# One product in place of two for z: the sum of phi(k) folded to 64 partitions, its bf16 high and low parts stacked

## Chip, cores, metric

The kernel runs on one core of a Trainium2 chip. The metric is the device time of one execution in microseconds. Before and after a change are compared by runs on the same chip. All runs told here are of one core and "fast" (within 1.5% of the fastest run of the same kernel).

Engines in the profile: PE is TensorE's matmul, PEld its weight load, DVE is VectorE, ACT is ScalarE, POOL is GpSimd, SP is SyncE, which issues the DMAs.

## The reference

Linear attention with 32 heads of 16, and a gated FFN, both of the same x (2048 x 512), mixed by a sigmoid gate. What matters here is the sum z of phi(k) over all tokens, which only the denominator uses:

```python
phi = lambda t: jnp.where(t > 0, t + 1, jnp.exp(t)) + 1e-6
pq, pk = phi(q), phi(k)
kv = jnp.einsum("bhsd,bhse->bhde", pk, v)
z = jnp.einsum("bhsd->bhd", pk)                       # the sum over tokens
num = jnp.einsum("bhqd,bhde->bhqe", pq, kv)
den = jnp.einsum("bhqd,bhd->bhq", pq, z)[..., None] + 1e-6
o = num / den
# a = o @ wo;  b = (silu(x @ w1) * (x @ w3)) @ w2;  out = g * a + (1 - g) * b
```

## The kernel before

The order of PE's instructions is set by hand, in the order of the text. All other engines are ordered automatically at compile time: each engine works through one queue in order, but which instruction stands where in that queue is chosen by a scheduler.

Four PSUM buffers in a pool called psM, used in rotation, carry the k tiles, the four q tiles of the first block, two r_ps (remainder of the FFN) and then gate_ps and up_ps of each FFN chunk. So r_ps 0 and 1 take the buffers of q tiles 0 and 1, the first gate_ps takes that of q tile 2, and the first up_ps that of q tile 3.

The names in the timelines: ScalarE reads r_ps as thr and upr. In an FFN chunk ScalarE makes th from gate_ps, VectorE makes gs from th and gate_ps, and then hT from gs and up_ps; with gs and hT the two buffers come free. For the denominator GpSimd multiplies pq by z_sb to qz, VectorE sums qz to den and inverts it to rden, GpSimd makes pqn from pq and rden, and a DMA transposes it to pqT, which the first o_ps reads.

```python
psM = ctx.enter_context(tc.tile_pool(name="psM", bufs=4, space=bass.MemoryType.PSUM))
# ... (cut: loads and constants)
def phi(dst, ps):                                     # frees ps only with its last line
    e = work.tile([P, D], BF16, tag="phi_e", name="phi_e")
    e_ins = nc.scalar.activation(out=e[:], in_=ps, func=ACT.Exp)
    em = work.tile([P, D], BF16, tag="phi_m", name="phi_m")
    nc.vector.tensor_scalar(out=em[:], in0=e[:], scalar1=1.0, scalar2=1e-6, op0=ALU.min, op1=ALU.add)
    nc.vector.scalar_tensor_tensor(out=dst, in0=ps, scalar=0.0, in1=em[:], op0=ALU.max, op1=ALU.add)
    return e_ins
# ... (cut)
def emit_k_phi(k_ps, t):                              # pks: partial sums, one per partition
    e_ins = phi(pk_sb[:, t, :], k_ps[:])
    if t == 0:
        nc.gpsimd.tensor_copy(pks[:], pk_sb[:, t, :])
    else:
        nc.gpsimd.tensor_add(pks[:], pks[:], pk_sb[:, t, :])
# ... (cut: transposes, k tiles, XP products, the q, r, FFN and output emitters)
emit_q(0, 2, psM, "mm")
emit_q(0, 3, psM, "mm")
emit_rem(0, 0, psM, "mm")
emit_rem(0, 1, psM, "mm")
# ... (cut: kvT_ps and its masked copy)
pks_hi = consts.tile([P, D], BF16, name="pks_hi")
nc.gpsimd.tensor_copy(pks_hi[:], pks[:])
pks_lo = consts.tile([P, D], BF16, name="pks_lo")
nc.gpsimd.tensor_sub(pks_lo[:], pks[:], pks_hi[:])
for fc in range(FC):                                  # ten FFN chunks of the first block
    emit_ffn(0, fc)
    if fc == 0:
        z_ps = psX.tile([P, D], FP32, tag="XP1", name="z_ps")
        nc.tensor.matmul(z_ps[:], lhsT=ones_b[:], rhs=pks_hi[:], start=True, stop=False)
        nc.tensor.matmul(z_ps[:], lhsT=ones_b[:], rhs=pks_lo[:], start=False, stop=True)
        nc.scalar.activation(out=z_sb[:], in_=z_ps[:], func=ACT.Copy)
    if 1 <= fc <= TPB:
        emit_den(0, fc - 1)                           # qz on GpSimd, its reduction on VectorE
    if fc == TPB + 1:
        emit_norm(0)                                  # rden on VectorE, pqn on GpSimd, pqT by DMA
    # ... (cut: W_ps after chunks 1 and 3, in the buffers XP0 to XP3)
```

## Time and profile before

| | value | where it is read |
|---|---|---|
| time | 181.27 us (181.25 to 181.48, 3 runs) | the runs |
| span of the profiled run | 179.2 us | profile page |
| PE busy | 174.8 us, 98% | profile page |
| one 128x512 product | 0.216 us (0.86 us for four) | chain of waits |
| stretch from the third q tile to the first o_ps | 24.37 us | timeline of PE |

The stretch in the last row is the part of the program that the change touches. I measure it from the start of the products of q tiles 2 and 3 (one line of the timeline) to the start of the first o_ps. It leaves out what comes before: the stretch starts between 35.07 and 36.04 us in the twelve traces, and where I looked the difference arose in the first 12 us, in waits of PE for the loads of x.

The profile page of before, first part (busy microseconds, share of the span, instructions):

```profile
span 179.2 us, 2463 instructions
PE 174.8 (98%) x884; PEld 83.7 (47%) x884; DVE 118.0 (66%) x202; ACT 65.8 (37%) x123; POOL 61.4 (34%) x69
```

VectorE's last step of phi, which frees the PSUM buffer, for tiles 1 and 2:

```profile
36.62 0.68 DVE L143 SCALAR_TENSOR_TENSOR pq<-q_ps,phi_m 128x512 bf16<-128x512 f32 x1
37.53 0.69 DVE L143 SCALAR_TENSOR_TENSOR pq<-q_ps,phi_m 128x512 bf16<-128x512 f32 x1
```

Tile 1 is free at 36.62 + 0.68 = 37.30 us, and the second r_ps, eight products after the first, follows at about 37.5 us (36.83 and half of 1.36). So its slack is 0.2 us. Tile 2 is free at 38.22 us and the first gate_ps starts at 39.08: 0.9 us.

The same stretch cut in three by busy time of each engine (first the r products and kvT, then the ten FFN chunks, then q and r of the next block up to the first o_ps):

```profile
35.10:39.08 3.98, 3.98 (x41) 3.04 (x40) 3.91 (x9) 3.22 (x8) 1.94 (x3) 1.00 0.31 97
39.08:57.93 18.85, 18.81 (x90) 8.40 (x88) 16.81 (x34) 9.02 (x17) 9.72 (x10) 1.00 0.19 34
57.93:59.47 1.54, 1.54 (x13) 1.06 (x12) 1.34 (x2) 0.48 (x1) 0.00 (x0) 1.00 0.17 35
```

The columns are the window, its length, then PE, PEld, DVE, ACT and POOL, the granted clock, DMA share and GB/s. In the chunks VectorE works 16.81 of 18.85 us, and PE loses about 0.3 us to it. One reason is visible in VectorE's timeline, before, at the start of the chunks:

```profile
41.61 0.69 DVE L317 TENSOR_TENSOR hT<-up_ps,gs 128x512 bf16<-128x512 f32 x1
43.31 0.69 DVE L222 TENSOR_REDUCE den<-qz 128x32 f32<-128x512 f32 x1 [1.01 <-POOL qz L219]
43.91 0.68 DVE L314 SCALAR_TENSOR_TENSOR gs<-th,gate_ps 128x512 bf16<-128x512 bf16 x1
```

The scheduler put the first den ahead of gs of chunk 1. VectorE waits 1.01 us for qz, and for the last 0.4 us of that the gs could have run (its th ends at 42.90 us); it starts at 43.91.

### The profile page before, as it was taken

To read this page: it belongs to the slowest core of one execution; us is meant where nothing else is said; L and a number is where in the kernel's file an instruction comes from. 1 tells how busy PE (TensorE), PEld (TensorE's weight loads), DVE (VectorE), ACT (ScalarE), POOL (GpSimd) and SP (SyncE) were. 2 spreads that over 40 slices of the span, in tenths; PEclk is the share of its full clock that TensorE was granted. 3 is DMA by queue.
4 is the path that set the end of the run, shared out by engine and by line. 5 is a ranking of instruction groups with operands and counts; after the bars stand their busy time and mean duration, and the time that the engine had idled before them with its cause. 6 is when DMAs were issued, how large, how long until landed. Compare 5 with 4: busy or idle time off the path is not lost.

```text
span 179.2 us, 2463 instructions
## 1 busy us (share of the span) xinstructions
PE 174.8 (98%) x884; PEld 83.7 (47%) x884; DVE 118.0 (66%) x202; ACT 65.8 (37%) x123; POOL 61.4 (34%) x69
## 2 busy tenths in 40 slices
PE   8899999999999999999999999999999999999993
PEld 3344444474444545444445444444545444444463
DVE  1388667897998837398787374977764669776000
ACT  3442322566523334343324343332443323331221
POOL 5177765646453323253003232620032328100000
PEclk9999999999999999999999999999999999999999
DMA  5999999901006011115000101240001013300011
GB/s 165 244 242 239 294 334 398 348 28 26 9 11 110 0 44 33 44 42 104 0 0 4 44 31 42 59 90 5 0 7 54 19 59 67 61 0 0 29 46 45
DMA packets 29340, 15.14 MB, mean 84 GB/s; under 512 B 20656, under 2 KB 28304, under 8 KB 29328
## 3 DMA queue, kind: packets, MB, share of 16 engines
q1 hardware_dynamic: 29328, 14.98, 31.2%
q8 instruction: 7, 0.11, 0.3%
q14 instruction: 5, 0.04, 0.1%
HBM read 8.42 MB, written 2.10 MB: 59 GB/s over the span
## 4 chain that ended last, share of the span: by engine, by line
PE 93%; DVE 2%; DMA 2%; SPq 1%; ACT 0%; issue 0%; DVEq 0%
PE o_ps L344 19%; PE gate_ps L301 18%; PE up_ps L307 18%; PE o_ps L335 8%; PE q_ps L211 8%; PE XP L198 8%; PE k_ps L178 6%; PE r_ps L235 3%; PE o_ps L339 2%; DMA x_sb<-in_A_x_dram 2%; PE k L178 2%; DVE hT L317 1%; DVE gs L314 1%; PE kvT_ps L402 0%; SPq L86 0%; PE W_ps L429 0%
## 5 line engine op out<-in xcount | busy, mean ns | idle before, releaser
L301 PE MATMUL gate_ps<-xT,w_sb 128*128 128x512 bf16 x160 | 41.1, 379 | 0.0
L307 PE MATMUL up_ps<-xT,w_sb 128*128 128x512 bf16 x160 | 41.1, 379 | 0.0
L219 POOL TENSOR_TENSOR qz<-pq,z_sb 128x512 f32<-128x512 bf16 x16 | 18.5, 1162 | 60.2 <-DVE pq L143 58.6
L312 ACT ACTIVATE th<-gate_ps 128x512 bf16<-128x512 f32 x40 | 23.9, 597 | 38.2 <-PE gate_ps L301 37.8
L344 PE MATMUL o_ps<-w_sb,hT 128*128 128x512 bf16 (+2 forms) x180 | 37.5, 355 | 0.0
L314 DVE SCALAR_TENSOR_TENSOR gs<-th,gate_ps 128x512 bf16<-128x512 bf16 x40 | 27.3, 682 | 5.9 <-ACT th L312 5.6
L317 DVE TENSOR_TENSOR hT<-up_ps,gs 128x512 bf16<-128x512 f32 x40 | 27.7, 691 | 3.8
L140 DVE TENSOR_SCALAR phi_m<-phi_e 128x512 bf16<-128x512 bf16 x32 | 14.4, 450 | 23.0 <-ACT phi_e L138 22.9
L344 PEld LDWEIGHTS <-hT 128*128 128x128 bf16 x180 | 16.8, 97 | 17.9
L307 PEld LDWEIGHTS <-w_sb 128*128 128x128 bf16 x160 | 15.6, 98 | 19.0 <-issue 0.2
L301 PEld LDWEIGHTS <-w_sb 128*128 128x128 bf16 x160 | 15.6, 98 | 18.9 <-issue 0.3
L349 ACT ACTIVATE o_out<-o_ps,omg 128x512 bf16<-128x512 f32 (+2 forms) x17 | 11.1, 656 | 30.4 <-PE o_ps L344 30.4
L284 POOL TENSOR_TENSOR pqn<-pq,rden 128x512 bf16<-128x512 bf16 x16 | 16.6, 1056 | 14.1 <-DVE rden L277 11.7
L188 POOL TENSOR_TENSOR pks<-pks,pk_sb 128x512 f32<-128x512 f32 x15 | 17.6, 1173 | 8.9 <-DVE pk_sb L143 8.4
L222 DVE TENSOR_REDUCE den<-qz 128x32 f32<-128x512 f32 x16 | 10.9, 684 | 8.9 <-POOL qz L219 8.8
L335 PE MATMUL o_ps<-W_sb,pqT 128*128 128x512 bf16 (+2 forms) x72 | 16.8, 355 | 0.0
L211 PE MATMUL q_ps<-wq_sb,xT 128*128 128x512 bf16 x64 | 16.3, 379 | 0.0
L198 PE MATMUL XP<-pk_sb,x_sb 128*128 128x512 bf16 x64 | 16.1, 379 | 0.0
L138 ACT ACTIVATE phi_e<-k_ps 128x512 bf16<-128x512 f32 x12 | 7.2, 597 | 15.3 <-PE k_ps L178 15.3
L178 PE MATMUL k_ps<-wk_sb,xT 128*128 128x512 bf16 x48 | 12.3, 379 | 0.0
L138 ACT ACTIVATE phi_e<-q_ps 128x512 bf16<-128x512 f32 x16 | 9.6, 597 | 7.0 <-PE q_ps L211 6.8
L143 DVE SCALAR_TENSOR_TENSOR pq<-q_ps,phi_m 128x512 bf16<-128x512 f32 x16 | 11.1, 691 | 0.5
(59 smaller groups left out, 116.5 us busy)
## 6 DMA issues: line engine op xcount, KB each, us to landing
w_sb<-in_B_w_dram SPq DMA_DIRECT2D x3, 1280.0 KB, 9.6
out_dram<-o_out SPq DMA_DIRECT2D x15, 128.0 KB, 1.9
x_sb<-in_A_x_dram SPq DMA_DIRECT2D x3, 512.0 KB, 4.3
wk_sb<-in_A_wqkv_dram SPq DMA_DIRECT2D x2, 256.0 KB, 3.0
wq_sb<-in_A_wqkv_dram SPq DMA_DIRECT2D x1, 512.0 KB, 4.9
wv_sb<-in_A_wqkv_dram SPq DMA_DIRECT2D x1, 512.0 KB, 6.6
wo_sb<-in_A_wo_dram SPq DMA_DIRECT2D x1, 512.0 KB, 10.5
x_sb<-in_A_x_dram SPq DMA_DIRECT2D x2, 128.0 KB, 2.7
```

The source lines that it names most:

```text
L178: nc.tensor.matmul(k_ps[:], lhsT=xT[:, kc, t * P : (t + 1) * P], rhs=wk_sb[:, kc, :], start=(kc == 0), stop=(kc == KC - 1),)
L188: nc.gpsimd.tensor_add(pks[:], pks[:], pk_sb[:, t, :])
L198: nc.tensor.matmul(XP_ps[dc][:], lhsT=x_sb[:, t, dc * P : (dc + 1) * P], rhs=pk_sb[:, t, :], start=(t == 0), stop=(t == NT - 1),)
L211: nc.tensor.matmul(q_ps[:], lhsT=xT[:, kc, ts_tok], rhs=wq_sb[:, kc, :], start=(kc == 0), stop=(kc == KC - 1),)
L219: nc.gpsimd.tensor_tensor(out=qz[:], in0=st[tb, "pq"][:, tt, :], in1=z_sb[:], op=ALU.mult)
L301: nc.tensor.matmul(gate_ps[:], lhsT=w1_sb[:, kc, fsl], rhs=xT[:, kc, tok_sl], start=(kc == 0), stop=(kc == KC - 1),)
L307: nc.tensor.matmul(up_ps[:], lhsT=w3_sb[:, kc, fsl], rhs=xT[:, kc, tok_sl], start=(kc == 0), stop=(kc == KC - 1),)
L312: nc.scalar.activation(out=th[:], in_=gate_ps[:], func=ACT.Tanh, scale=0.5)
L314: nc.vector.scalar_tensor_tensor(out=gs[:], in0=th[:], scalar=1.0, in1=gate_ps[:], op0=ALU.add, op1=ALU.mult)
L317: nc.vector.tensor_tensor(out=st[tb, "hT"][:, fc, :], in0=up_ps[:], in1=gs[:], op=ALU.mult)
L335: nc.tensor.matmul(o_ps[:], lhsT=st[tb, "pqT"][:, c, tsl], rhs=W_sb[:, c, a:b], start=(c == 0), stop=False,)
L344: nc.tensor.matmul(o_ps[:], lhsT=st[tb, "hT"][:, fc, tsl], rhs=w2_sb[:, fc, a:b], start=False, stop=(fc == FC - 1),)
```

## The change

The intent is to save one of two z products on PE. The 128 partial sums per column are first added in pairs, in fp32, to 64; their bf16 high part then fills partitions 0 to 63 of one tile and their low part partitions 64 to 127, so one product with ones sums both. Two copies from one half of the partitions to the other are needed, and are given to ScalarE. As the chain is longer, z comes after chunk 2 instead of chunk 0, and den and norm move two chunks with it.

```diff
-    pks_hi = consts.tile([P, D], BF16, name="pks_hi")
-    nc.gpsimd.tensor_copy(pks_hi[:], pks[:])
-    pks_lo = consts.tile([P, D], BF16, name="pks_lo")
-    nc.gpsimd.tensor_sub(pks_lo[:], pks[:], pks_hi[:])
+    HP = P // 2
+    pks_up = consts.tile([HP, D], FP32, name="pks_up")
+    nc.scalar.activation(out=pks_up[:], in_=pks[HP:P, :], func=ACT.Copy)
+    pks_f = consts.tile([HP, D], FP32, name="pks_f")
+    nc.gpsimd.tensor_add(pks_f[:], pks[0:HP, :], pks_up[:])
+    pks_hl = consts.tile([P, D], BF16, name="pks_hl")
+    nc.gpsimd.tensor_copy(pks_hl[0:HP, :], pks_f[:])
+    pks_lo = consts.tile([HP, D], BF16, name="pks_lo")
+    nc.gpsimd.tensor_sub(pks_lo[:], pks_f[:], pks_hl[0:HP, :])
+    nc.scalar.activation(out=pks_hl[HP:P, :], in_=pks_lo[:], func=ACT.Copy)
     for fc in range(FC):
         emit_ffn(0, fc)
-        if fc == 0:
+        if fc == 2:
             z_ps = psX.tile([P, D], FP32, tag="XP1", name="z_ps")
-            nc.tensor.matmul(z_ps[:], lhsT=ones_b[:], rhs=pks_hi[:], start=True, stop=False)
-            nc.tensor.matmul(z_ps[:], lhsT=ones_b[:], rhs=pks_lo[:], start=False, stop=True)
+            nc.tensor.matmul(z_ps[:], lhsT=ones_b[:], rhs=pks_hl[:], start=True, stop=True)
             nc.scalar.activation(out=z_sb[:], in_=z_ps[:], func=ACT.Copy)
-        if 1 <= fc <= TPB:
-            emit_den(0, fc - 1)
-        if fc == TPB + 1:
+        if 3 <= fc <= TPB + 2:
+            emit_den(0, fc - 3)
+        if fc == TPB + 3:
             emit_norm(0)
```

## The prediction

> **What bounds the kernel.** TensorE. The page gives PE busy 174.8 us of a 179.2 us span (98%); the chain of waits is PE for 93% of the span, at a granted clock of 0.998 (view of cores). The measured 181.27 us is 2.1 us more than the span. In the chain four 128x512 matmuls take 0.86 us, so one costs 0.216 us; the 379 ns that the groups list overlaps the neighbours. The Trainium skill, "TensorE: Matmul & The Clock Gate", section "Wait — 56ns, not 53.3ns?", has 215.7 ns start to start; this trace agrees.
>
> In the timeline of the first block's ten FFN chunks (39.2 to 58.1 us) PE is packed but for about 0.3 us: up_ps of chunk 4 starts 0.95 us after its gate_ps instead of 0.865, and gate_ps of chunk 6 comes 1.07 us after the product before it. The chain shows why: VectorE (hT, gs, rden from 47.5 to 51.0 us) frees PSUM buffers late, since four den reductions (0.68 us each, 0.6 apart) and the normalisation (1.4 us) come on top of 1.39 us of gs and hT per 1.73 us chunk.
>
> **Removed.** One of the two z products: 0.216 us of PE, on the critical path. That is the only sure gain.
>
> **Added, off PE.** Two ScalarE copies of 64x512 (0.60 us each, as every 128x512 ACTIVATE here) and a GpSimd add of 64x512 (I expect 1.15 us, as for 128 partitions: each lane keeps its 512 elements). The cast (0.61) and the subtraction (1.16) stay as long. The chain from pks (complete at 35.3 us) was 1.85 us long and ended at 37.2; z waited to 40.8 only for its place in PE's order. It becomes 0.6 + 1.15 + 0.61 + 1.16 + 0.6, with hand-overs 4.5 us, ending near 40 us if each step starts at once, near 44 us if ScalarE and GpSimd (two hr products, 1.05 us) are busy. The product now comes at about 44.7 us. I expect PE not to wait for it.
>
> **Moved.** z_sb lands at about 45.7 instead of 42.0 us, so qz, den, rden and pqn move 3.7 us later. VectorE's extra work meets chunks 3 to 7 instead of 1 to 5. The same load on the same four PSUM buffers: PE's 0.3 us of stalls probably moves two chunks later and changes by 0.3 us either way. Before, pqT's first transpose was issued at 52.3 us and landed 2.4 us later, 4.7 us before o_ps first read it (59.4). Afterwards I expect landing at 58.4 and need at 59.1: 0.7 us is left. Later slices are needed 4 us apart and made 1.1 us apart.
>
> ScalarE's queue is in order: if the last copy (waiting for GpSimd) stands ahead of a th, that th comes up to 1 to 2 us late, against about 1.2 us of slack before PE lacks a PSUM buffer. That could give back 0.2 to 0.7 us.
>
> **Prediction.** 181.27 - 0.22 + about 0.05 for the risks: 181.1 us, 8 in 10 between 180.8 and 181.7. Faster by over 2%: 0.005; within 2%: 0.985; slower by over 2%: 0.01.
>
> **What would show it.** Right: one z product fewer, PE busy down about 0.2 us; PE not waiting for pks_hl; copies near 0.6 us and the half-partition add near 1.15 us; den and rden 3.5 to 4 us later; o_ps not waiting for pqT. Wrong: half-partition operations clearly shorter; PE idle before z, before gate_ps of chunks 3 to 8, or before o_ps.
>
> **What would make it wrong.** A th stuck behind the last copy for over 1.5 us; pqT landing after 59.1 us, which adds its lateness once; the first block's chunks stalling over 0.3 us longer because den and rden bunch up; or the other engines' order changing elsewhere (they are scheduled automatically).

## More of the kernel before

The timeline of PE, before, around the q tiles (start, duration, engine, line, operation, out<-in, shapes, count; a bracket at the end would give idle time and its releaser):

```profile
35.10 1.89 PE L211 MATMUL q_ps<-wq_sb,xT 128*128 128x512 bf16 x8
36.83 1.53 PE L235 MATMUL r_ps<-wr_sb,xT 128*128 128x193 bf16 x16
38.19 1.05 PE L402 MATMUL kvT_ps<-XP_sb,wv_sb 128*128 128x128 bf16 x16
39.08 1.03 PE L301 MATMUL gate_ps<-xT,w_sb 128*128 128x512 bf16 x4
```

No bracket: PE has no wait here. The timeline of ScalarE over the same time:

```profile
34.44 0.60 ACT L138 ACTIVATE phi_e<-q_ps 128x512 bf16<-128x512 f32 x1 [1.13 <-PE q_ps L211]
...
36.16 0.60 ACT L138 ACTIVATE phi_e<-q_ps 128x512 bf16<-128x512 f32 x1
37.02 0.60 ACT L138 ACTIVATE phi_e<-q_ps 128x512 bf16<-128x512 f32 x1 [0.27 <-PE q_ps L211]
```

These are the exponentials of q tiles 1, 2 and 3; each starts as soon as its tile is there.

## The result and the profile after

The time after is 183.97 us (median of 4 runs, 183.64 to 184.18), beside 181.38 us before (4 runs, 181.25 to 181.73). The ratio is 1.0138 with a 95% interval of 1.0122 to 1.0154. Ratios here are the mean time of one kernel's fast runs over that of the other's fast runs of the same rounds, so they are not quite the ratios of the medians. The change makes the kernel about 2.5 us slower, where 0.2 us less was predicted, and the time lies outside the stated range.

The profile page, first part, after:

```profile
span 182.5 us, 2464 instructions
PE 175.0 (96%) x883; PEld 83.5 (46%) x883; DVE 117.1 (64%) x202; ACT 66.6 (37%) x125; POOL 62.7 (34%) x70
```

One PE instruction is gone, as meant, but the span grew by 3.3 us. PE's busy time did not fall, so busy time alone would not have shown the saved product either. The timeline of PE, after, for the same place:

```profile
35.59 1.89 PE L211 MATMUL q_ps<-wq_sb,xT 128*128 128x512 bf16 x8
37.32 0.84 PE L235 MATMUL r_ps<-wr_sb,xT 128*128 128x193 bf16 x8
39.16 0.84 PE L235 MATMUL r_ps<-wr_sb,xT 128*128 128x193 bf16 x8 [1.00 <-DVE pq L143]
39.84 1.05 PE L402 MATMUL kvT_ps<-XP_sb,wv_sb 128*128 128x128 bf16 x16
42.04 1.02 PE L301 MATMUL gate_ps<-xT,w_sb 128*128 128x512 bf16 x4 [1.15 <-DVE pq L143]
```

Two waits of over 1 us have appeared, both for pq, that is for the PSUM buffers of q tiles 1 and 2. The idle time in brackets is a little less than the loss, because the ends of matmuls are modelled. From start to start, the r products take 39.84 - 37.32 = 2.52 us instead of 1.36, and from kvT_ps to gate_ps it is 2.20 us instead of 0.89: a loss of 1.16 and of 1.31 us. Both come well before the z product. The timeline of ScalarE, after, says why:

```profile
35.79 0.63 ACT L413 ACTIVATE pks_up<-pks 64x512 f32<-64x512 f32 x1 [2.00 <-POOL pks L188]
36.33 0.57 ACT L138 ACTIVATE phi_e<-q_ps 128x512 bf16<-128x512 f32 x1
...
39.69 0.63 ACT L420 ACTIVATE pks_hl<-pks_lo 64x512 bf16<-64x512 bf16 x1 [1.82 <-POOL pks_lo L419]
40.34 1.08 ACT L138 ACTIVATE phi_e<-q_ps 128x512 bf16<-128x512 f32 x2
```

The first new copy stands ahead of the exponential of q tile 1, and the second ahead of those of tiles 2 and 3, although the text has both after all four. ScalarE sits idle for 2.00 and 1.82 us, waiting for GpSimd. For the last 0.86 us of the first wait (q tile 1 is there at about 34.93 us, if it takes 1.07 us from the start of its products as before) and for all of the second, finished q tiles wait behind it.

VectorE's timeline shows that the first loss has a second part:

```profile
36.94 0.98 DVE L140 TENSOR_SCALAR phi_m<-phi_e 128x512 bf16<-128x512 bf16 x1 [0.88 <-ACT phi_e L138]
...
38.44 0.67 DVE L143 SCALAR_TENSOR_TENSOR pq<-q_ps,phi_m 128x512 bf16<-128x512 f32 x1
```

The phi_m of tile 1 took 0.62 us before and takes 0.98 us here, while GpSimd works on pks_f (36.50 to 37.76 us; e4 comes back to such overlaps). So my estimate is that about 0.36 of the 1.16 us comes through GpSimd's work on the fold; no run tests that part alone. The chain of waits of after follows the whole path (start, duration, what; "issue" pieces and some steps between are left out):

```profile
34.61 1.16 POOL pks L188
35.79 0.64 ACT pks_up L413
36.50 1.27 POOL pks_f L415
38.51 1.16 POOL pks_lo L419
40.34 0.60 ACT phi_e L138
41.30 0.70 DVE pq L143
42.04 1.02 PE gate_ps L301 x4
```

The fold's chain ends with the second copy at 40.32 us and feeds a product that comes at 47.65 us, so its data are 7 us early. It has become part of the critical path through a queue and not through its data. Note that the chain reaches gate_ps without passing through r_ps: the first stall of PE lies beside it.

The stretch in three windows, after:

```profile
35.59:42.04 6.45, 4.31 (x41) 3.09 (x40) 3.67 (x7) 4.40 (x11) 3.18 (x4) 1.00 0.24 76
42.04:60.89 18.85, 18.67 (x86) 8.28 (x86) 17.05 (x35) 9.31 (x19) 7.46 (x8) 1.00 0.04 9
60.89:62.68 1.79, 1.71 (x13) 1.00 (x12) 1.46 (x4) 0.65 (x2) 1.25 (x2) 1.00 0.38 75
```

The first window is 2.47 us longer. The ten chunks take 18.85 us as before, although a product of 0.22 us is gone: the later den and norm cost that much more in waits for VectorE. The last is 0.25 us longer, as the first o_ps waits for pqT. In all 27.09 instead of 24.37 us: 2.72 us more. The profiled span has another 0.5 us at the start of the program (the transposes of the second token tile on PE at 6.00 instead of 5.51 us, waiting for the DMA of x_sb), which the change doesn't touch.

### The profile page after: what moved, and what is told of

Its sections match the earlier page's. It is cut to its first block, busy times and chain, and to the rows that moved or that the text cites. A ratio compares the mean times of both kernels' runs of the same rounds, so it can differ in the third digit from the quotient of the medians.

```text
span 182.5 us, 2464 instructions
## 1 busy us (share of the span) xinstructions
PE 175.0 (96%) x883; PEld 83.5 (46%) x883; DVE 117.1 (64%) x202; ACT 66.6 (37%) x125; POOL 62.7 (34%) x70
## 4 chain that ended last, share of the span: by engine, by line
PE 81%; DVE 6%; POOL 4%; DMA 3%; issue 2%; ACT 2%; SPq 1%; DVEq 0%; ACTq 0%; POOLq 0%
PE o_ps L344 19%; PE gate_ps L301 16%; PE up_ps L307 16%; PE o_ps L335 8%; PE XP L198 7%; PE k_ps L178 6%; PE q_ps L211 5%; DMA x_sb<-in_A_x_dram 2%; PE o_ps L339 2%; PE r_ps L235 2%; DVE gs L314 2%; PE k L178 2%; DVE hT L317 1%; DMA pqT<-pqn 1%; DVE den L222 1%
```

## The experiments

Theory Q is the reading above: two ScalarE copies stand in an in-order queue ahead of the exponentials, and this costs about 2.5 us. Its rivals are theory L, that moving z, den and norm two chunks later costs the time, and theory R, that the longer chain or GpSimd's work on 64 partitions does. All ten kernels gave a correct output within the tolerance of the comparison.

In the table, the columns "r and kvT" to "to o_ps" are differences of the three windows of the stretch against before (3.98, 18.85 and 1.54 us), read from the timeline of PE.

| kernel | r and kvT | ten chunks | to o_ps | stretch | ratio of times (95%) |
|---|---|---|---|---|---|
| the change | +2.47 | 0.00 | +0.25 | 27.09 | 1.0138 (1.0122 to 1.0154) |
| e1: new chain, z early | +2.47 | -0.22 | +0.01 | 26.63 | 1.0126 (1.0100 to 1.0152) |
| e2: old chain, z late | +0.01 | +0.21 | +0.25 | 24.84 | 1.0015 (0.9997 to 1.0033) |
| e3: copies on GpSimd, z late | 0.00 | -0.01 | +0.24 | 24.60 | 1.0018 (1.0000 to 1.0036) |
| e4: copies on GpSimd, z early | 0.00 | +0.19 | +0.01 | 24.57 | 0.9988 (0.9973 to 1.0003) |
| e5: second copy behind | +1.16 | 0.00 | +0.24 | 25.77 | 1.0073 (1.0057 to 1.0088) |
| e6: both copies behind | 0.00 | +0.86 | +0.24 | 25.47 | 1.0075 (1.0054 to 1.0095) |
| e7: high part alone | 0.00 | -0.22 | +0.01 | 24.16 | 0.9987 (0.9972 to 1.0002) |
| e8: e7 and den behind hT | 0.00 | -0.50 | +0.01 | 23.88 | 0.9969 (0.9955 to 0.9983) |
| e9: before and den behind hT | +0.01 | -0.29 | 0.00 | 24.09 | 0.9990 (0.9973 to 1.0006) |
| e10: e4 and den behind hT | +0.01 | -0.51 | +0.01 | 23.88 | 0.9992 (0.9977 to 1.0007) |

### e1: the change with z, den and norm back at their old places

```diff
-        if fc == 2:
+        if fc == 0:
             z_ps = psX.tile([P, D], FP32, tag="XP1", name="z_ps")
# ... (cut: the product and its copy, unchanged)
-        if 3 <= fc <= TPB + 2:
-            emit_den(0, fc - 3)
-        if fc == TPB + 3:
+        if 1 <= fc <= TPB:
+            emit_den(0, fc - 1)
+        if fc == TPB + 1:
             emit_norm(0)
```

> The change with its new chain (fold, two ScalarE copies, one product) kept, but the z product put back after FFN chunk 0 and den and norm back where they were. Theory Q (the two ScalarE copies stand in ScalarE's in-order queue ahead of the phi exponentials of q tiles 1, 2 and 3, and PE loses 1.16 us before the second r_ps and 1.31 us before the first gate_ps because the q tiles' PSUM buffers come back late): both stalls stay, only the 0.25 us wait of o_ps for pqT goes; 183.5 to 183.9 us, about 2.3 us above before. Theory L (the z product two chunks later delays den and norm, and this costs the time): about 181.2 us, no slower than before.

It took 183.50 us (before on the same chip 181.46). Both stalls are there to within a hundredth of a microsecond, and the wait of o_ps is gone. Almost the whole loss remains without the move, so theory L falls as the main cause. The ten chunks now show the saved product, -0.22 us.

### e2: the kernel before with only the move

```diff
-        if fc == 0:
+        if fc == 2:
             z_ps = psX.tile([P, D], FP32, tag="XP1", name="z_ps")
# ... den and norm two chunks later, as in the change
```

> The kernel before with its own chain (cast and subtraction of 128 partitions on GpSimd, two products, no ScalarE copies), only the z products moved to chunk 2 and den and norm moved two chunks later, as in the change. Theory Q: no stall before r_ps or gate_ps; only o_ps may wait some tenths for pqT; 181.3 to 181.8 us. Theory L: about 184 us, as the change.

It took 181.77 us beside 181.46. The stretch has grown by 0.47 us: 0.21 us in the chunks, 0.25 us before the first o_ps. The ratio of the times, 1.0015, agrees with that in size, but its interval just includes 1. So the move costs something, nearly half a microsecond in the trace, and it is not the 2.5 us.

### e3: the change with the copies on GpSimd

```diff
-    nc.scalar.activation(out=pks_up[:], in_=pks[HP:P, :], func=ACT.Copy)
+    nc.gpsimd.tensor_copy(pks_up[:], pks[HP:P, :])
# ... (cut: pks_f, the cast and pks_lo, unchanged)
-    nc.scalar.activation(out=pks_hl[HP:P, :], in_=pks_lo[:], func=ACT.Copy)
+    nc.gpsimd.tensor_copy(pks_hl[HP:P, :], pks_lo[:])
```

> The change with the two 64-partition copies moved from ScalarE to GpSimd (0.6 us each), everything else as in the change. ScalarE's order of phi exponentials is then that of before. Theory Q: no stall before r_ps and gate_ps, one product saved, o_ps may wait 0 to 0.3 us for pqT: 181.1 to 181.5 us. A rival R (the longer dependent chain itself, or GpSimd's half-partition work, delays PE): 183 to 184 us. If a copy between partition halves does not work on GpSimd the output will be wrong; then only the time counts.

It took 181.77 us beside 181.46, a little over the expected range. The fold, the chain and the half-partition work are all still there, in the same order, and the two stalls are gone. Only the engine of the two copies differs. Theory R falls as the main cause, and theory Q stands. In this trace GpSimd's sum is complete about half a microsecond earlier against PE than in the change; in e4, with the same copies, it is not, and the two stalls are gone there too. PE's timeline of this run:

```profile
37.21 1.53 PE L235 MATMUL r_ps<-wr_sb,xT 128*128 128x193 bf16 x16
38.58 1.06 PE L402 MATMUL kvT_ps<-XP_sb,wv_sb 128*128 128x128 bf16 x16
39.47 1.03 PE L301 MATMUL gate_ps<-xT,w_sb 128*128 128x512 bf16 x4
```

and GpSimd's:

```profile
35.24 0.61 POOL L413 COPY pks_up<-pks 64x512 f32<-64x512 f32 x1
...
39.30 0.60 POOL L420 COPY pks_hl<-pks_lo 64x512 bf16<-64x512 bf16 x1
```

The chain ends at 39.90 us, before the old place of z. The kernel is still not faster than before, because the later den and norm take back what the product saved (chunks -0.01, o_ps +0.24).

### e4: copies on GpSimd, and z after chunk 0

The edit is that of e3 and that of e1 together.

> As the GpSimd copies, and the z product back after chunk 0. The chain on GpSimd should end near 39.7 us from pks at 35.3 (0.65 + 1.2 + 0.65 + 1.2 + 0.65) and z is wanted near 41.0, so PE should not wait. The one saved product is then the only difference: 0.22 us less than before, 181.1 to 181.25 us, ratio 0.9988. If PE waits for the chain: 181.4 us or more.

It took 181.32 us beside 181.46; the interval of the ratio includes 1. The median is what was expected, but the trace does not support the reason given: the chunks are 0.19 us longer than before, not 0.22 us shorter. The agreement counts for little, as the profiled run (181.50 us) is among the slowest of the six. The stalls have grown by about 0.4 us. VectorE starts later: its phi_m of the last q tile took 1.20 us while GpSimd worked on pks_lo. In before, the same phi_m took 0.28 us, with GpSimd idle (from 37.18 to 39.49 us). First before, then e4:

```profile
38.13 0.28 DVE L140 TENSOR_SCALAR phi_m<-phi_e 128x512 bf16<-128x512 bf16 x1
```

```profile
38.40 1.20 DVE L140 TENSOR_SCALAR phi_m<-phi_e 128x512 bf16<-128x512 bf16 x1
```

The Trainium skill, "SBUF — State Buffer", section "SBUF: two separate sides", says that GpSimd and some VectorE operations share a pair of ports as an exclusive lock, so that one of them blocks for the other's whole instruction. The 1.20 us agrees with that: pks_lo ran from 38.30 to 39.45 us, and phi_m from 38.40 to 39.60. In this trace the first gs then starts at 42.09 us (before, at 40.85; the stretch starts 0.27 us later here). One extra stall can be read off: pq of q tile 3 ends at 40.32 us, and the first up_ps, which takes its buffer, starts at 40.38, 0.17 us late. That the lateness makes the other extra stalls too is my reading; e10 bears on it.

### e5: only the second copy put behind the r products' activations

The block's last upr activation is kept (its instruction in `st[0, "upr_ins", 1]`), and the copy is ordered behind it on ScalarE, without a wait of its own:

```diff
-    nc.scalar.activation(out=pks_hl[HP:P, :], in_=pks_lo[:], func=ACT.Copy)
+    with tc.issue_after(st[0, "upr_ins", 1].ins):
+        nc.scalar.activation(out=pks_hl[HP:P, :], in_=pks_lo[:], func=ACT.Copy)
```

> The change, with only ScalarE's second copy (pks_hl from pks_lo) ordered behind the last upr of the first block, so behind the phi exponentials of q tiles 2 and 3; the first copy stays ahead of the exponential of q tile 1. Theory Q, with the two waits adding up: the stall before the second r_ps (1.2 us, first copy) stays, the one before the first gate_ps (1.3 us, second copy) goes; 182.4 to 183.0 us. If one copy alone causes all: 184 us or 181.6 us.

It took 182.52 us beside 181.25. The timeline of PE in this run (its line numbers are two higher where the edit shifted them):

```profile
36.85 0.84 PE L235 MATMUL r_ps<-wr_sb,xT 128*128 128x193 bf16 x8
38.70 0.84 PE L235 MATMUL r_ps<-wr_sb,xT 128*128 128x193 bf16 x8 [1.00 <-DVE pq L143]
39.38 1.05 PE L404 MATMUL kvT_ps<-XP_sb,wv_sb 128*128 128x128 bf16 x16
40.27 1.03 PE L303 MATMUL gate_ps<-xT,w_sb 128*128 128x512 bf16 x4
```

The stall of the first copy is unchanged and that of the second is gone (0.89 us from kvT_ps to gate_ps, as before). So the first copy's place alone costs 1.16 us, and the second's adds 1.31 us to it. It does not follow that taking away the first stall alone would give back 1.16 us: in the change, the chain that holds gate_ps runs through the fold and the second copy and not through r_ps, so by that trace the second copy's place would cost the whole 2.47 us by itself. No run tests this.

### e6: both copies behind

The edit is that of e5 for both copies.

> The change, with both ScalarE copies ordered behind the last upr of the first block. The scheduler then puts the second copy between th of chunk 0 and th of chunk 1, with GpSimd's hr products between the steps of the fold. Theory Q: no stall before r_ps and the first gate_ps, but th of chunk 1 is held until about 44.4 us, W_sb of chunk 1 after it until about 46.1, and z_ps (which reuses that PSUM buffer) with it: PE loses 1.0 to 1.7 us there instead; 182.2 to 183.0 us. If it is only the two exponential waits that cost, and ScalarE's queue has slack later: 181.5 to 181.8 us.

It took 182.76 us beside 181.25; PE loses 0.85 us before z_ps (46.48 instead of about 45.63 us) where 1.0 to 1.7 us was expected. ScalarE's timeline:

```profile
44.19 0.63 ACT L424 ACTIVATE pks_hl<-pks_lo 64x512 bf16<-64x512 bf16 x1 [2.51 <-POOL pks_lo L422]
44.85 0.60 ACT L314 ACTIVATE th<-gate_ps 128x512 bf16<-128x512 f32 x1
45.34 1.08 ACT L441 ACTIVATE W_sb<-W_ps 128x512 bf16<-128x512 f32 x2
```

and PE's:

```profile
44.77 1.03 PE L309 MATMUL up_ps<-xT,w_sb 128*128 128x512 bf16 x4
46.48 0.39 PE L429 MATMUL z_ps<-pks_hl,ones_b 128*128 128x512 bf16 x1 [0.68 <-ACT W_sb L441]
```

The two old stalls are gone, and a new one stands at z: the second copy, waiting for GpSimd, holds th of chunk 1 and W_sb behind it, and z reuses the PSUM buffer of W_ps. This is the risk that the prediction named, a th stuck behind the last copy; it is real, but in the change itself it does not occur. Moving a waiting instruction along an in-order queue only chooses who waits behind it.

### e7: the saved product alone

For this run the low part is left out of the kernel before, which is a lower precision on purpose.

```diff
-    pks_lo = consts.tile([P, D], BF16, name="pks_lo")
-    nc.gpsimd.tensor_sub(pks_lo[:], pks[:], pks_hi[:])
# ... (cut)
-            nc.tensor.matmul(z_ps[:], lhsT=ones_b[:], rhs=pks_hi[:], start=True, stop=False)
-            nc.tensor.matmul(z_ps[:], lhsT=ones_b[:], rhs=pks_lo[:], start=False, stop=True)
+            nc.tensor.matmul(z_ps[:], lhsT=ones_b[:], rhs=pks_hi[:], start=True, stop=True)
```

> The kernel before with the low part and its product left out: one product of pks_hi for z (z then rounded like a sum of bf16 values; a smaller precision on purpose), no copies, no fold, z still after chunk 0. This is the saved product alone. Theory: 0.22 us less, 181.15 to 181.3 us where before is at 181.4, ratio 0.9988; PE's span from the third q tile to the first o_ps down from 24.37 to about 24.15 us, unless VectorE's lateness in the chunks takes some of it.

It took 180.98 us beside 181.25. The stretch is 0.21 us shorter, as one product would have it. The ratio agrees, but 0.13% is inside what six runs can resolve: its interval includes 1. So the prize of the change is confirmed in the trace at about 0.2 us and no more.

### e8, e9, e10: VectorE's order

In all three, den and norm of the first block are ordered behind hT of their own chunk on VectorE, so that the first den no longer stands ahead of a ready gs.

```diff
# ... (cut: hT's instruction of each chunk is kept in st[tb, "hT_ins", fc])
-            emit_den(0, fc - 1)
+            with tc.issue_after(st[0, "hT_ins", fc].ins):
+                emit_den(0, fc - 1)
         if fc == TPB + 1:
-            emit_norm(0)
+            with tc.issue_after(st[0, "hT_ins", fc].ins):
+                emit_norm(0)
```

e8 applies it to e7:

> As the run with the high part alone, and the first block's four den reductions and the normalisation ordered behind hT of their own chunk on VectorE (the automatic order puts the first den ahead of gs of chunk 1, where VectorE waits 1.0 us for qz with that gs ready). If the 0.3 us of PE stalls in chunks 4 and 6 come from that wait, they shrink: another 0.1 to 0.3 us, 180.9 to 181.2 us where before is at 181.4. If they come from the sheer sum of VectorE's work, nothing changes against the run with the high part alone.

e9 applies it to the kernel before:

> The kernel before with nothing changed but VectorE's order: den and norm of the first block behind hT of their own chunk. If the 0.3 us of stalls come from VectorE waiting for qz ahead of a ready gs, the stretch from the third q tile to the first o_ps falls from 24.37 to about 24.1 us, and the time by 0.2 to 0.3 us: 180.95 to 181.2 where before is at 181.3. If the gain of the last run came with the missing low part, nothing changes.

e10 applies it to e4:

> The fold and the one product of high and low part as in the change, copies on GpSimd, z after chunk 0, and den and norm behind hT of their own chunk: a version with the change's arithmetic. GpSimd's copies lengthen one phi_m on VectorE to 1.2 us and first gs starts 1.2 us later than before, which cost 0.3 us of stalls in chunks 0, 3 and 4 in the run without the den order; with it I expect the stretch near 24.0 to 24.3 us (before 24.37) and 180.9 to 181.3 us where before is at 181.3.

e8 took 180.72 us beside 181.25, e9 180.85 beside 181.03, and e10 181.07 beside 181.03. In all three the ten chunks run without a stall in PE's timeline, and the stretch falls by 0.49, 0.28 and 0.49 us. VectorE's timeline of e8 at the place shown of before:

```profile
42.69 0.69 DVE L314 SCALAR_TENSOR_TENSOR gs<-th,gate_ps 128x512 bf16<-128x512 bf16 x1 [0.42 <-ACT th L312]
43.48 0.69 DVE L317 TENSOR_TENSOR hT<-up_ps,gs 128x512 bf16<-128x512 f32 x1
44.09 0.68 DVE L222 TENSOR_REDUCE den<-qz 128x32 f32<-128x512 f32 x1
```

The 1.01 us wait has gone and gs runs first. The order alone (e9) is worth 0.28 us of the trace, so the 0.3 us of stalls in before did come from it and not from the sum of VectorE's work, which is the same. The edit moves all four den and the norm at once, so the first den's place is not tested apart from the others'.

e10, with e4's copies on GpSimd and a phi_m of 1.20 us too, has no stall either. But its trace is not e4's with only the order mended: GpSimd's sum of phi(k) was complete 0.31 us before the start of the stretch, in e4 0.17 us after it. So q tile 3's buffer came back in time (pq ends at 40.56 us, up_ps starts at 40.77), and of the 0.70 us between the chunks of e4 and e10, the 0.17 us at the first up_ps is not the order's doing; that stall comes before any den.

In times, only e8 is resolved from before: 0.31% faster, interval 0.17 to 0.45%. It is the fastest of all the kernels tried, at lower precision of z. e10 keeps the change's arithmetic and has the same stretch, but its time is not resolved from before: 0.49 us would be a ratio of 0.9973, just outside the interval. Its profiled run is the slowest of its six, and its stretch starts 0.82 us later than in before. 0.33 us of this arose at the transposes of the second token tile (5.84 us instead of 5.51), and a further wait of 0.31 us stands at 10.87 us, for the transposed load of x; there the text of the program is that of before. Whether that is chance, and how often the stall of e4's first up_ps appears in other executions, I did not settle.

## Why the prediction was wrong

**Right.** The kernel is PE bound and the product is worth 0.22 us (e7: 0.21 us of the stretch). The copies take 0.63 us (0.60 predicted), the GpSimd add on 64 partitions 1.26 us (1.15 predicted), the cast and the subtraction 0.60 and 1.15 us: half the partitions save nothing. The chain ends at 40.32 us in the trace, "near 40 us if each step starts at once". PE does not wait for pks_hl at z. The chunks' stalls changed by 0.2 us, inside the 0.3 us allowed "either way".

**Named as a risk, but not expected.** For pqT "0.7 us is left" was foreseen; o_ps waited 0.25 us instead (e2, e3). The den reductions came 3.7 us later as predicted, but the last step of rden 4.8 us later and not 3.7 (e3: 56.12 us against 50.89, less the 0.39 us by which that trace's chunks start later), and pqT with it.

**The step that failed** is "That could give back 0.2 to 0.7 us", and with it the assumption on where the copies stand in ScalarE's queue. The prediction counted the copies' duration as "off PE", took only a th of the FFN as what could stand behind a copy, and gave it "about 1.2 us of slack". I had read the text's order (copies after the r products) as the queue's order. The runs show the copies ahead of the exponentials of q tiles 1, 2 and 3, where the slack in before was 0.2 us and 0.9 us. The term stands at 1.16 + 1.31 = 2.47 us (e5 removes the second part, e3 and e4 both) in place of the 0.05 us in the sum. The prediction did name "the other engines' order changing elsewhere" as a thing that would make it wrong, but gave it no size, and neither r_ps nor the first gate_ps was on its list of places where PE might idle.

"Ending near 40 us if each step starts at once, near 44 us if ScalarE and GpSimd are busy" was a fair estimate of a chain that had time until 47.65 us. It missed that an early start of such a chain is bought with ScalarE standing still. The Trainium skill, "Perfetto Trace Analysis", section "Tensor Engine Instruction (MATMUL, LD_WEIGHTS)", notes that ScalarE's, VectorE's and GpSimd's queues are strict first in, first out. The traces agree: for 0.86 and 1.82 us ScalarE was idle with finished q tiles behind.

Why the scheduler chose these places was not tested. Its order is fixed at compile time, so it must go by something other than the waits seen on the chip.

**What is left.** The gain of 0.22 us was also cancelled by the move of z (e3: stretch +0.23 us without the ScalarE stalls; e2: +0.47 us for the move alone). With the copies on GpSimd and z early (e4), later stalls in the chunks took it back, one of them behind the long phi_m and the others in chunks 3, 4 and 6. With VectorE's order mended too (e10), the stretch is 0.49 us shorter than before, of which the order alone gives 0.28 us (e9).

## What to carry to other kernels

Before putting an operation that waits for another engine on an engine with "free" time, ask what stands behind it in that engine's queue, in the order that is really issued, and how late each of those may come before a buffer runs out. An instruction that waits in an in-order queue can cost its wait on top of its duration: the exponential of q tile 1 came 1.40 us late behind a copy of 0.63 us. Where engines are ordered automatically, compare the compiled order of the changed kernel with that of the old one before trusting a schedule read from the text, and give such an operation to an engine on which nothing urgent follows.

## What the Trainium skill lacked or had wrong

- "GPSIMD Engine Reference": it describes each of its cores as owning 16 partitions in ordinary compute, and, beyond a warning about reading what another of its cores has just written, doesn't say whether a plain copy may read one half of the partitions and write the other. Here it did: 64x512 from partitions 64 to 127 to partitions 0 to 63 in fp32 took 0.61 us, the way back in bf16 0.60 us, with a correct output (e3).
- "ScalarE: Activation LUTs", section "What ACT_TABLE_LOAD costs": 186 ns + 0.833 ns per element with immediate scale and bias makes an estimate of 613 ns for 512 elements; the passage does not tell sources apart. The runs show 597 ns for the exponentials from PSUM and 627 to 629 ns for the 64x512 copies from SBUF. The copies differ from the exponentials in more than the source, so which of it counts is not shown.
- No page that I read warns that an order chosen at compile time can put a waiting instruction ahead of urgent ones in an engine's queue, against the program text. Several stress that the queues are in order, and one speaks of instructions scheduled out of program order, but for sequences on VectorE that keep state. Here that difference was worth 2.47 us of a 24.37 us stretch.
